# Copies of k's last keys move from ScalarE to GpSimd, with six weight loads behind them in GpSimd's queue

## The chip, the cores and the metric

The kernel runs on one core of a Trainium2 chip. The metric is the device time of one execution in microseconds (us). Engines are named as the profile names them: PE is TensorE's matmul, PEld its weight load, DVE VectorE, ACT ScalarE, POOL GpSimd, SP SyncE. SP, ACT and POOL can issue DMAs; SPq, ACTq and POOLq are their queues. L331 is line 331 of the kernel before.

## What is computed

An attention with a threshold over 8 batches, 8 heads, 576 positions and 64 channels, in float32, and after it a feed-forward over all 4608 rows:

```
scores = q k^T / 8;  thresh = max(scores) - tau      (per row)
scores = where(scores >= thresh, scores, -1e9)
attn = softmax(scores);  a = attn v
x = a with heads side by side: (4608, 512)
h = x w_in;  g = h * sigmoid(1.702 h);  out = g w_out   (w_in 512 x 2048, w_out 2048 x 512)
```

The weights arrive in float64. The core has to make float32 of them itself.

## The kernel before, in words

**Pairs.** Two heads of a batch are worked together, so there are 32 pairs, counted from 0. A pair's 576 keys are four tiles of 128 and a tail of 64. For the four tiles the scores of each head are products of its own (`scores`, L350). For the tail both heads share one product: `prep_kd` (L331) copies the last 64 keys of each head's transposed k into the two diagonal 64x64 blocks of `kd`, a 128x128 tile whose other blocks were zeroed once at the start (L597), and the product with `kd` (L343) gives the tail scores of both heads. There is a single `kd`, so the copies of a pair wait until the tail product of the pair before has read it.

**A pair's way.** SP issues 4 DMAs for q and 4 for k of 72 KB each (`load_qk`, L220; for pair 0 ACT issues k's) and 4 for v (`load_v`, L230 and L234). q and k are read in rows of 32 floats, and their buffers are single; pairs 1 and 3 have buffers of their own inside `gT`, so names like gT<-in_q_dram or gT<-ps are theirs. DVE transposes q and k (`prep`, L326). PE makes the scores, ACT copies them out of PSUM (`keep`, L369), DVE takes the maxima in groups (`in_groups`, L383), folds them (L389 to L423) into one row. For the first eight pairs SP writes that row to DRAM (`row_out`, L435) and reads it back into all partitions as `mb` and `mbt` (`row_in`, L444 and L446). DVE subtracts it (`sub`, L453, L455), ACT masks and takes the exponential (L464, L468), PE multiplies by v (`values`) and, for the first five pairs, by ones for the sums (`sums_by_pe`, both L482), DVE divides (L511 to L532) and places the result in `xT` (L549).

**Weights.** There are 32 pieces of 128x512, 16 of w_in and 16 of w_out. POOL issues two DMAs of 512 KB for each (`load_w`, L278 and L279; the second is shifted by three bytes), and DVE and ACT make float32 of a piece in four steps: the exponent on DVE (`cv_ex`, L289), a power of two on ACT (`cv_power`, L297), the fraction on DVE (`cv_frac`, L303, L307), the product on DVE (`cv_end`, L315). Pieces are staged in parts of `w_out` that are free until later, or in two pairs of buffers w64; each load waits for its place to be given back by a `cv_end`, once the six places have been used.

**Feed-forward.** For blocks of 512 rows PE makes 16 tiles of h (`mm1`, L561), ACT a tanh (L569), DVE the gate (L572), then PE the second product (`mm2`, L580), ACT halves it (L587) and SP stores it. Its matmuls fill PE between the pairs' work, and the last blocks follow after the last pair.

**The order.** The order on each engine is fixed when the program is built. Each step is a `task` with an engine, a supposed cost, a rank, the tasks it comes `after`, and the pools it takes and gives. `run_in_order` plays these with supposed times and writes each engine's instructions in the order in which they would start. What an engine waits for on the chip is another thing: an instruction waits there only for data that it reads or overwrites, and for the instructions ahead of it on its engine. So the loads of pieces 0 to 5, which overwrite nothing that anyone still reads, are placed after a transpose in the plan (the lines with `w_loads` below), and on the chip have only the order of POOL before them. A planned wait holds the chip only where something ahead on the same engine really waits.

On POOL that order is, before: memsets, the load of tau, then the 32 weight loads. On ACT each pair's two copies stand ahead of its score copies or among them.

```
        if n in (2, 3):

            for a in w_loads[3 * (n - 2) : 3 * (n - 1)]:
                tasks[a][5].append(pk)
        pd = task("ACT", 0.5, r, prep_kd, n, after=[pk], take=("kd",))
```

`pk` is the transpose of k, `pd` the copies into `kd`; `tasks[a][5]` is the list of what load `a` comes after.

Of the kernel before, what the change touches and what calls it, by code (L numbers as in the profile page):

```python
# [30 lines left out]
def kernel(  # L31
# [29 lines left out]
    nc = tc.nc  # L61
# [29 lines left out]
    kd = const.tile([P, P], FP32, name="kd")  # L91
# [15 lines left out]
    tasks = []  # L107
# [26 lines left out]
    def task(engine, cost, rank, f, *a, after=(), take=(), give=(), lag=0.06):  # L134
        if 0 <= rank < LAST:
            rank += CV.get(f.__name__, 0.0) + (EARLY if a[0] < 2 * NPAIR else LATER).get(f.__name__, 0.0)
        tasks.append((engine, cost, rank, f, a, [x for x in after if x is not None],
                      take, give, lag))
        return len(tasks) - 1
# [67 lines left out]
    def own(n, *pools):  # L207
        return tuple(x + "_apart" for x in pools) if n in APART else pools
# [119 lines left out]

    def prep_kd(n):
        for h in range(2):  # L330
            nc.scalar.copy(  # L331
                out=kd[ts(h, D), ts(h, D)], in_=mats[n, 1][ts(h, D), MAIN:S]
            )

# [298 lines left out]
    for i in range(len(pieces)):  # L633
# [6 lines left out]
        a = task("POOL", 2.4, rank, load_w, i, after=w_loads[-1:], take=place, lag=5.0)  # L640
# [3 lines left out]
        a = task("DVE", 1.14, rank, cv_frac, i, after=[e])  # L644
# [47 lines left out]
    for n in range(NP):  # L692
        gate = per_pair * (n - LEAD)
        after = ffn[gate : gate + 1] if gate >= 0 else []
        r = float(n)
# [6 lines left out]
        lv = task("SP", 2.1, r - 1.2, load_v, n, take=("v_m", v_tail), lag=2.0)  # L702
        pq = task("DVE", 0.77, r, prep, n, 0, after=[lq], take=own(n, "qkT0"), give=own(n, "raw0"))
        pk = task("DVE", 0.77, r, prep, n, 1, after=[lk], take=own(n, "qkT1"), give=own(n, "raw1"))
        if n in (2, 3):

            for a in w_loads[3 * (n - 2) : 3 * (n - 1)]:
                tasks[a][5].append(pk)
        pd = task("ACT", 0.5, r, prep_kd, n, after=[pk], take=("kd",))
        mx = []  # L710
        for t in range(NKT + 1):
            tail = t == NKT
            copies = []
            for c in range(1 if tail else 2):

                a = task(
                    "PE", (0.97 if tail else 0.53) * slow, r, scores, n, t, c,
                    after=[pq, pk] + ([pd] if tail else []) + after,
                    take=("psA", "s_t") if tail else ("psA",) + (own(n, "s_m") if c == 0 else ()),
                    give=own(n, "qkT0", "qkT1") + ("kd",) if tail else (),  # L720
                )
                after = [a]
                copies.append(task("ACT", 0.65, r, keep, n, t, c, after=[a], give=("psA",)))
            mx.append(task("DVE", 0.76 if tail else 1.37, r, in_groups, n, t, ALU.max, after=copies))
        a = task("DVE", 0.78, r, over_tiles, n, ALU.max, after=mx)
        a = task("DVE", 0.78, r, over_groups, n, ALU.max, after=[a])
        if n < BY_DMA:
            a = task("DVE", 0.5, r, lower_rows, n, after=[a, tau_done], take=("row",))
            a = task("SP", 0.35, r, row_out, n, after=[a], lag=2.8)
# [4 lines left out]
        else:  # L734
            a = task("DVE", 0.7, r, lower, n, after=[a, tau_done])
            m = task("DVE", 1.38, r, spread_max, n, after=[a], take=own(n, "mb"))
        ws, subs = [], [m]
        for t in range(NKT + 1):
            tail = t == NKT
            a = task(  # L740
                "DVE", (0.76 if n < BY_DMA else 1.5) if tail else 1.36, r, sub, n, t, after=subs[-1:],
                give=own(n, "mb") + (("mbt",) if n < BY_DMA else ()) if tail else (),
            )
            subs.append(a)
            a = task("ACT", 0.68 if tail else 1.16, r, mask, n, t, after=[a])
# [3 lines left out]
        if n < NPAIR:  # L749

            pv = den = None
            for t in every:
# [3 lines left out]
                    take=("psM", "psM") if first else (),  # L756
# [3 lines left out]
                    take=("psA",) if first else (), give=(back[t],) if t < NKT else ("s_t", "v_m", v_tail),  # L760
                )
            a = task("DVE", 1.22, r, one_row, n, after=[den], give=("psM", "psM"))
        else:
            pv = task("PE", 4.85, r, values, n, every, after=ws + [lv], take=("psA",), give=("v_m", v_tail))
        if NPAIR <= n < BY_PE:
            a = task("PE", 5.2, r, sums_by_pe, n, every, False, after=ws + [pv], take=("psA",), give=back)
            a = task("DVE", 1.22, r, one_row, n, after=[a], give=("psA",))
        elif n >= BY_PE:
# [4 lines left out]
            a = task("DVE", 0.78, r, over_tiles, n, ALU.add, after=su + [pv], give=back)  # L773
            a = task("DVE", 0.78, r, over_groups, n, ALU.add, after=[a])
            a = task("DVE", 0.7, r, one_group, n, after=[a])
        a = task("DVE", 1.07, r, spread_sums, n, after=[a], take=("rc",))
# [41 lines left out]
```

## Time and profile before

| what | value |
|---|---|
| runs shown | 1429.61, 1431.24, 1432.67 us (median 1431.24) |
| the profiled execution | 1432.38 us; its span from the first to the last instruction 1430.5 us |
| mean granted clock of TensorE | 0.989 |
| PE busy | 1383.7 us (97%) |
| DVE busy | 970.2 us (68%) |
| ACT busy | 662.9 us (46%) |
| POOL busy | 36.8 us (3%) |
| copies into kd on ACT | 128, median 0.243 us |
| weight loads, issue on POOL | 64 DMAs, about 0.54 us each |
| weight loads, issue to landing | 8.4 us (median of w_in's first parts) |
| q and k loads of SP, issue to landing | 2.2 and 2.3 us (medians) |

The profile is of one execution. Busy time is the time in which an engine carried out instructions; an idle engine that is not on the path to the end costs nothing. A line of the timeline or of the chain of waits gives the start and the length in us; where several instructions stand in one line, the length reaches over all. "SPq L220" in the chain means that the path went through SP's issuing of that DMA. In the rows of the DMA queues a share is the time that packets took, of the time of all 16 DMA engines.

### The profile page before, as it was taken

The numbers are of one execution on the slowest core, as the hardware profiler recorded it, in microseconds if no ns is written. First come the engines' busy times: TensorE is split into PE (matmuls) and PEld (weight loads), VectorE is DVE, ScalarE is ACT, GpSimd is POOL, SyncE is SP. The second block draws the span as 40 slices with busy tenths as digits, with TensorE's granted clock in tenths as the row PEclk, the third lists the DMA queues.
The fourth block names the chain that finished last, engine by engine and source line by source line (L and its number), as shares of the span: only waits on it lengthen the run. The fifth ranks groups of instructions, "written<-read, shape, count | busy, mean of one in ns | idle before, by whom it ended". The sixth has DMA issues, their size and how long they took to land.

```text
span 1430.5 us, 13702 instructions
## 1 busy us (share of the span) xinstructions
PE 1383.7 (97%) x4936; PEld 652.2 (46%) x4936; DVE 970.2 (68%) x1629; ACT 662.9 (46%) x886; POOL 36.8 (3%) x78
## 2 busy tenths in 40 slices
PE   4779999999999999999999999999999999999998
PEld 2434444444444444444444444444444444444443
DVE  3999899988878887788788887888778710100200
ACT  3786555755555555555555555555445500100100
POOL 2012210000000000000000000000000000000000
PEclk8899999999999999999999999999999999999999
DMA  9476962211111111111111111111110000000000
GB/s 246 92 216 219 308 199 65 74 26 25 33 40 33 26 25 40 40 25 25 33 40 33 26 25 40 41 25 25 33 40 8 1 7 22 0 7 22 0 7 22
DMA packets 205707, 79.31 MB, mean 55 GB/s; under 512 B 192840, under 2 KB 192840, under 8 KB 205640
## 3 DMA queue, kind: packets, MB, share of 16 engines
q1 hardware_dynamic: 196072, 44.60, 14.5%
q0 software_dynamic: 7200, 33.55, 6.5%
q8 instruction: 39, 0.64, 0.2%
q10 hardware_dynamic: 2368, 0.30, 0.2%
q14 instruction: 28, 0.23, 0.1%
HBM read 68.93 MB, written 9.47 MB: 55 GB/s over the span
## 4 chain that ended last, share of the span: by engine, by line
PE 88%; DVE 6%; SPq 2%; DMA 2%; ACT 2%; issue 1%; DVEq 0%; ACTq 0%
PE ops L580 34%; PE hps L561 34%; PE pv L482 9%; PE ps L350 8%; PE ps L343 2%; SPq L220 2%; DVE part L383 1%; DVE s_m L453 1%; DMA mb<-row 1%; ACT gT L468 0%; DVE gT L453 0%; PE den L482 0%; DMA row<-flat 0%; ACT gT L464 0%; DVE part_t L383 0%
## 5 line engine op out<-in xcount | busy, mean ns | idle before, releaser
L561 PE MATMUL hps<-xT,w_in 128*128 128x512 f32 x1152 | 505.7, 595 | 1.9 <-DVE gT L572 1.9
L580 PE MATMUL ops<-w_out,gT 128*128 128x512 f32 x1152 | 506.6, 595 | 0.0
L383 DVE TRANSPOSE_TENSOR_REDUCE part<-s_m 128x36 f32<-128x1152 f32 x228 | 303.9, 1360 | 98.9 <-ACT s_m L369 92.2
L561 PEld LDWEIGHTS hps<-xT,w_in 128*128 128x128 f32 x1152 | 216.3, 190 | 269.4 <-issue 254.3
L580 PEld LDWEIGHTS ops<-w_out,gT 128*128 128x128 f32 x1152 | 216.1, 190 | 268.3 <-issue 265.9
L572 DVE SCALAR_TENSOR_TENSOR gT<-th,hps 128x512 f32<-128x512 f32 x144 | 97.7, 678 | 234.7 <-ACT th L569 233.9
L369 ACT COPY s_m<-ps 128x576 f32<-128x576 f32 x240 | 139.2, 651 | 173.0 <-PE ps L350 171.7
L569 ACT ACTIVATE th<-hps 128x512 f32<-128x512 f32 x144 | 85.3, 592 | 205.7 <-PE hps L561 194.0
L464 ACT ACTIVATE s_m<-s_m 128x1152 f32<-128x1152 f32 x120 | 138.6, 1155 | 72.5 <-DVE s_m L453 72.3
L468 ACT ACTIVATE s_m<-s_m,shift,scl 128x1152 f32<-128x1152 f32 x120 | 161.8, 1348 | 2.9
L453 DVE TENSOR_TENSOR s_m<-s_m,mb 128x1152 f32<-128x1152 f32 x120 | 156.4, 1351 | 7.1 <-DMA mb<-row 6.5
L350 PE MATMUL ps<-qkT 64*128 64x288 f32 x960 | 144.8, 433 | 13.7 <-DVE qkT L326 12.2
L350 PEld LDWEIGHTS ps<-qkT 64*128 64x128 f32 x960 | 84.0, 190 | 91.6 <-issue 51.5
L482 PE MATMUL pv<-s_m,v_m 128*64 128x288 f32 x960 | 124.2, 411 | 0.0
L587 ACT ACTIVATE osb<-ops 128x512 f32<-128x512 f32 x36 | 21.4, 593 | 220.8 <-PE ops L580 220.8
L482 PEld LDWEIGHTS pv<-s_m,v_m 128*64 128x64 f32 x960 | 67.1, 137 | 63.4 <-issue 10.7
L383 DVE TRANSPOSE_TENSOR_REDUCE part_t<-s_t 128x18 f32<-128x576 f32 x59 | 44.1, 747 | 1.6 <-ACT s_t L369 0.8
L549 DVE TENSOR_TENSOR xT<-pv,rc 128x288 f32<-128x288 f32 (+8 forms) x96 | 28.4, 352 | 17.3 <-PE pv L482 16.6
L343 PE MATMUL ps<-qkT,kd 128*128 128x288 f32 x120 | 36.9, 430 | 0.0
L482 PE MATMUL pv<-s_t,v_t 128*64 128x288 f32 x256 | 36.5, 406 | 0.0
L458 DVE TENSOR_TENSOR s_t<-s_t,mb 64x576 f32<-64x576 f32 x48 | 36.0, 750 | 0.3
L427 DVE STREAM_TRANSPOSE mb<-thr 128x1152 f32<-128x1152 f32 x24 | 33.1, 1378 | 0.8
(81 smaller groups left out, 611.8 us busy)
## 6 DMA issues: line engine op xcount, KB each, us to landing
out_dram<-osb SPq DMA_DIRECT2D x36, 256.0 KB, 2.0
q_raw<-in_q_dram SPq DMA_DIRECT2D x120, 72.0 KB, 2.2
k_raw<-in_k_dram SPq DMA_DIRECT2D x116, 72.0 KB, 2.3
v_m<-in_v_dram SPq DMA_DIRECT2D x64, 128.0 KB, 2.3
w_out<-in_moe_w_in_dram POOLq DMA_DIRECT2D x12, 512.0 KB, 8.4
w<-in_moe_w_out_dram POOLq DMA_DIRECT2D x12, 512.0 KB, 5.7
w_out<-in_moe_w_in_dram POOLq DMA_DIRECT2D x12, 511.6 KB, 9.2
w64s<-in_moe_w_out_dram POOLq DMA_DIRECT2D x12, 511.6 KB, 6.8
```

Of the source, the lines that this page charges most:

```text
L343: nc.tensor.matmul(ps[:, i, 0:SH], lhsT=kd, rhs=qT[:, ts(i, SH)], start=True, stop=True,)
L350: nc.tensor.matmul(ps[:, h, 0:SH], lhsT=kT[ts(h, D), ts(t, P)], rhs=qT[ts(h, D), ts(c, SH)], start=True, stop=True,)
L369: nc.scalar.copy(out=o, in_=pss.pop((n, t, c))[:, :, 0:SH])
L383: nc.vector.tensor_reduce(out=o, in_=i, axis=AXL.X, op=op, apply_transpose=True)
L453: nc.vector.tensor_tensor(out=s, in0=s, in1=mb, op=ALU.subtract)
L464: nc.scalar.activation(out=s, in_=s, func=AF.Prelu, alpha=STEEP)
L468: nc.scalar.activation(out=s, in_=s, func=AF.Exp, scale=scl, bias=shift)
L482: nc.tensor.matmul(o[c][ts(h, D), 0:SH], lhsT=lhsT, rhs=rhs, start=(t == 0), stop=(t == NKT),)
L561: nc.tensor.matmul(hidden[j], lhsT=w_in[:, c, ts(j, P)], rhs=xTs[blk][:, c, :], start=(c == 0), stop=(c == NDC - 1),)
L569: nc.scalar.activation(out=ths[j], in_=hidden[j], func=AF.Tanh, scale=GELU_SCALE / 2)
L572: nc.vector.scalar_tensor_tensor(out=gT[j], in0=ths.pop(j), scalar=1.0, in1=hidden.pop(j), op0=ALU.add, op1=ALU.mult)
L580: nc.tensor.matmul(acc[i], lhsT=gT[j][:, ts(i, P)], rhs=w_out[:, j, :], start=(j == 0), stop=(j == NFC - 1),)
```

## The change

`prep_kd` is carried out by POOL, as a tensor copy, in place of ACT. In the plan its task is one of POOL's, with the same supposed cost, and it is made ahead of the lines with `w_loads`; the loads of pieces 0 to 2 now come after the copies of pair 2, those of pieces 3 to 5 after the copies of pair 3, where they came after the transposes of k of these pairs.

```diff
     def prep_kd(n):
         for h in range(2):
-            nc.scalar.copy(
+            nc.gpsimd.tensor_copy(
                 out=kd[ts(h, D), ts(h, D)], in_=mats[n, 1][ts(h, D), MAIN:S]
             )
...
         pk = task("DVE", 0.77, r, prep, n, 1, after=[lk], take=own(n, "qkT1"), give=own(n, "raw1"))
+        pd = task("POOL", 0.5, r, prep_kd, n, after=[pk], take=("kd",))
         if n in (2, 3):
 
+
             for a in w_loads[3 * (n - 2) : 3 * (n - 1)]:
-                tasks[a][5].append(pk)
-        pd = task("ACT", 0.5, r, prep_kd, n, after=[pk], take=("kd",))
+                tasks[a][5].append(pd)
```

In the built program POOL's order becomes: memsets, tau, the copies of pairs 0, 1 and 2, the loads of pieces 0 to 2, the copies of pair 3, the loads of pieces 3 to 8, the copies of pair 4, pieces 9 to 18, pair 5, pieces 19 to 29, pair 6, pieces 30 and 31, and then the copies of pairs 7 to 31. The second copy of a pair waits for the first. PE's and SP's orders are the same as before. On DVE one reduction (L383) of pair 5 stands behind five instructions of weight conversion that it stood ahead of; on ACT one score copy changes places with one step of conversion; else only the copies are gone there.

## Prediction

> **What bounds the kernel now.** I read the busy time by stage first, because the shares of the whole span (PE 97%) hide where the 3% lies. The columns are the stretch, its length, busy time with instructions of PE, PEld, DVE, ACT and POOL, granted clock, DMA share, GB/s.
>
> ```profile
> 0.00:45.00 45.00, 21.12 (x104) 14.03 (x104) 18.82 (x32) 18.55 (x34) 8.26 (x26) 0.89 0.88 231
> 45.00:122.00 77.00, 60.81 (x390) 31.99 (x392) 73.83 (x133) 62.37 (x72) 10.61 (x20) 0.87 0.58 172
> 122.00:200.00 78.00, 76.15 (x232) 34.90 (x234) 70.81 (x124) 41.55 (x61) 17.89 (x32) 1.00 0.79 251
> 200.00:1150.00 950.00, 949.00 (x3562) 449.04 (x3560) 782.47 (x1304) 514.08 (x676) 0.00 (x0) 1.00 0.16 35
> ```
>
> From 122 us on PE is busy 1025 of 1028 us: nothing is to be had there. From 45 to 122 VectorE is full (73.8 of 77). In the first 45 us no engine is (PE 21, DVE 19, ACT 19), and the DMA share is 0.88. PE's idle time before 122 us is 23.9 + 16.2 = 40.1 us, the cap of any gain. What holds the head stands in the chain of waits up to 46 us (start, length, what):
>
> ```profile
> 6.62 0.70 SPq L220
> 7.32 0.04 issue
> 7.36 7.56 SPq L220
> 14.93 0.04 issue
> 14.97 6.59 SPq L220
> ...
> 26.11 2.38 DMA gT<-in_k_dram
> ...
> 37.75 1.67 DMA row<-flat
> 39.42 0.02 issue
> 39.44 5.32 DMA mb<-row
> ```
>
> SP needs 15.5 us, from 6.62 to 22.15, to issue the four q loads of pair 1 (pairs are counted from 0), where four loads of the next pair take 2.06. Everything on the head's path is behind SP's queue: pair 1's k, the row of pair 0's maxima, and its broadcast mb, on which DVE starts its first subtract at 44.78. The DMA queues say why. Two windows (queue, packets, MB, share of 16 engines), first 6 to 22 us, then 24 to 38:
>
> ```profile
> q0 software_dynamic: 1234, 5.75, 93.8%
> q1 hardware_dynamic: 1139, 0.28, 8.3%
> ```
>
> ```profile
> q1 hardware_dynamic: 13165, 1.78, 75.6%
> ```
>
> q0 holds POOL's weight loads, q1 SP's loads. Beside the weights q1 moves 1139 packets in 16 us, 71 a us; alone 13165 in 14 us, 940 a us. A 72 KB load of q or k is cut into 128 byte pieces, 576 of them: 0.6 us alone, 8 us beside the weights. The weights come that early because the first six loads wait for nothing but their queue (POOL's timeline: start, length, operation):
>
> ```profile
> 2.46 0.53 POOL L278 DMA_DIRECT2D w_out<-in_moe_w_in_dram  x1
> ```
>
> while DVE first touches them at 69 us (DVE's timeline, the first conversion):
>
> ```profile
> 69.05 0.39 DVE L289 TENSOR_SCALAR w_out<-w_out 128x512 uint32<-128x512 uint32 x1
> ```
>
> **The change part by part.** *The order.* Before, "after pk" tied the first loads to a DVE transpose in the planner alone: the order on POOL had nothing ahead of them, so they ran at 2.46. Now POOL's order is copies of pairs 0, 1, 2, loads 0 to 2, copies of pair 3, loads 3 to 5. Those copies wait for DVE's transpose of k and for the tail scores of the pair before (PE), and POOL works in order: the loads are now held on the chip.
>
> *Head without weights.* SP starts the q loads of pair 1 at 6.62 as before. From there to the row are 28 issues (q, k of pairs 1, 2, 3 and v of pair 1). From 26.71 to 37.75, without weights, 20 issues took 11.04, 0.552 each: 28 x 0.552 = 15.5, so SP is ready for the row at 22.1, not 37.75. Is the row's data there? The loads of pair 0 (4608 packets, two queues) at 940 a us from about 2 us are in by about 7; k was transposed at 11.35 before. PE then starts at about 7.5 (12.19 before), ACT's last score copy ends 9.0 later (12.19 to 21.20), 16.5; the last large reduction (1.34) and the fold from 31.84 to 34.70 (2.9) give 20.7. SP at 22.1 is last: **-15.6** for the row.
>
> *First burst.* Pair 2's transposes follow the fold in DVE's order (1.44), so its copies on POOL start at 22.2, also behind the tail scores of pair 1 (PE, about 7.5 + 2 x 8.3 = 24 at the pace of pairs 0 and 1, a score copy every 0.96 us; 21 if pair 2's pace, eight in 4.45, comes sooner). So loads 0 to 2 issue from 22.7 to 24.7 on; an issue at 2.46 became heavy traffic some 2.2 later (156 GB/s from 2.5 to 5 us, 253 and 335 in the next two stretches of 2.5), so at 25 to 27. They are 3.1 MB, at the 379 GB/s of the window from 6 to 22 us about 8.2 us. The row goes out at 22.1 and mb is issued at 23.8: the row escapes, mb does not. Prices from rows: row 1.67 alone and 4.28 beside weights (at 155.53), mb 5.32 alone and 7.33 beside weights (at 159.83). I take 1.7 + 7.3: mb at 31.1, not 44.75, **-13.7**. The ends are -15.6 (neither is hit) and -11.0 (both are).
>
> *Second burst.* Loads 3 to 5 come after the tail scores of pair 2, which end at 62.93 now: at 49.2, plus copies, 50 to 53, on the wires from 52 to 60.5. Beside them stand pair 5's loads, issued at 68.50 to 73.73 before, 55 to 60 now: mostly starved until 60.5, then 4.9 us for 4608 packets, to 65.4. The row of pair 2 (77.34, so 63.6) queues behind them on SP's queue, up to 1.8 late. Its cover: mb was issued at 78.57, took 3.7 (median of that window), and DVE came to it at 84.41, 2.1 later. So it may cost nothing; up to 5 if the cover is gone. I take **+0.7**.
>
> *Are the weights late?* Load 0 is due at 69.05, so 55.4, and lands by 36. Load 3 is due at 73.25, so 59.6; issued at 50, with 8.4 us to landing (median of these loads) at 58.4. It is covered by 1 us at worst; loads 4 and 5 are due at 97. What is late next there is load 3, at its lateness, on DVE.
>
> *The copies themselves.* 128 copies of 64x64 leave ACT: 128 x 0.243 = 31 us of 663. ACT is busy 514 of 950 us in the long stage and PE 949, so this is worth 0; the copies' own waiters lost 3.0 us in four places of PE's weight loads, with 1.0 us of PE idle in that stage: at most 1. The trace has no POOL copy: a POOL memset of 64x64 is 0.144, POOL's longest row 0.76. A pair costs 0.3 to 1.5; I take 0.5, as on ACT (the same shape). It is hidden wherever eight score products stand between the transpose and the tail (137.76 to 145.51 for pair 5). On POOL the copies stand behind loads: those of pair 5 behind load 18 (139.28, 6 us before PE wants them), of pair 6 behind load 29 (189.3, wanted at 215.3), of pair 7 behind load 31 (199.9, wanted at 242.4). In the other direction load 9 waits behind pair 4's copies, which wait for PE at 84.8; it went out at 97.80. All 0 now; without that cover each us is one of PE's.
>
> The Trainium skill speaks against this place: SBUF — State Buffer, section "Who interferes with whom", says that a DVE instruction with two SBUF inputs contends with a GpSimd instruction that reads SBUF, and that whoever comes second is fully blocked. No row here shows it. By the rule a copy could wait out one subtract (1.35 us, row of L453), or hold DVE for its own length: under 1 us in the head, and in the long stage against 6 us of cover; the sum would be -12, not -13.
>
> *DVE's order.* One reduction of pair 5 slides behind five instructions of weight conversion near 197 us, 2.9 us by their rows, with PE full: 0, at most 3.
>
> *Does the shift last?* DVE does the same work from the first subtract on and is full until 122 us; PE after that. Weight loads from the seventh on wait for DVE's conversions (65.8 us of POOL's waiting) and move with them. So the whole rest is moved forward.
>
> **Sum.** -13.7 + 0.7 = -13.0. The profiled execution took 1432.38 (span 1430.5): 1419.4. The median of the runs, 1431.24, lies 1.14 lower: **1418.2**.
>
> **Rivals.** (1) *The bursts cost more than I price.* For: 71 against 940 packets a us, and only 1 to 2 us of room on either side. If row and mb are both hit (-11.0) and the second burst costs its 5: -6 , 1425. Against: the weights need over 2 us from issue to traffic. (2) *The head's gain is covered up.* DVE could be stopped after 45 us by something that doesn't move: the conversions, fed by loads that now queue behind PE and DVE. For: POOL waits for both now. Against: only loads 0 to 5 changed, and they are due late. Time 1431. That the order doesn't hold the loads would also end here, but POOL has one queue. (3) *Slower: the starved queue.* If pair 3's last k load still has its 576 packets to move when the weights arrive, they need 8.1 us at 71 a us, ahead of row and mb; with both hit (+4.6) and pair 5's loads starved on the path for the whole second burst (+8.2) that is 20.9 against 15.6: +5.3, 1436.5. It decides at about 1.5 us: SP issues that load by 22, its packets go within 2, the weights come at 25 to 27. (4) *Better.* POOL's copies come late enough (27) to spare mb altogether, and cold products of pair 1 run at pair 2's pace: -17, 1414.
>
> **Chances.** Forecast (1415.5 to 1420.5) 0.66; rival (1), 1420.5 to 1426, 0.19; (4) 0.06; (2) 0.05; (3) 0.04. A measurement of this kernel tells 0.2% (2.9 us) from no change. Faster by more than that 0.91, within 0.05, slower 0.04. The range goes from 1414, the end without contention (-15.6) and the 1.6 by which the lowest run lies under the median, to 1425, the end of (1).
>
> **What would show it.** Right: in the changed profile the q loads of pair 1 take about 2 us on SP, first row at about 22, first subtract at 30 to 32, POOL's first weight load at 22 to 26, mb at 7 rather than 5 us, PE's idle before its first hps some 13 lower, the long stage unchanged. Wrong: a row or mb above 10 us, DVE idle ahead of a conversion (L289, L303), PE idle ahead of L343 with the copy as releaser, or a first subtract after 36.

## The result and the profile after

The changed kernel took 1425.13 us (median of four runs, 1422.51 to 1427.46) against 1431.36 for the kernel before: a ratio of 0.9957, interval 0.9933 to 0.9981. It is 6.2 us faster, where I forecast 13.0, and its time lies 0.1 above my range. In a later comparison of the same kernel (e8 below) the median was 1420.05 against 1432.57 for the kernel before, 12.5 us faster, and its runs went from 1416.72 to 1426.49. So this kernel's time is spread over 11 us, where those of the kernel before stay within 3 to 5, and the question has two parts: where do up to 12 us go, and why not in every run?

The profiled execution shown here is the slowest of the four, 1427.46 us with a span of 1425.7, against 1432.38 and 1430.5 before. First the busy time by stage, with the columns of the prediction (PE, PEld, DVE, ACT, POOL, granted clock, DMA share, GB/s):

```profile
0.00:45.00 45.00, 28.73 (x174) 16.98 (x176) 33.30 (x54) 27.71 (x38) 6.45 (x26) 0.92 0.84 181
45.00:122.00 77.00, 50.50 (x333) 25.46 (x330) 61.74 (x116) 51.73 (x61) 15.44 (x30) 0.89 0.71 214
122.00:200.00 78.00, 78.00 (x261) 36.33 (x261) 72.61 (x130) 39.25 (x55) 19.21 (x36) 1.00 0.80 261
```

The head did what was forecast: in the first 45 us DVE works 33.3 us instead of 18.8. But in the next stretch, where DVE was full (73.8 of 77), it now works only 61.7. Twelve us that the head won are lost there. The chain of waits says on what (start, length, what):

```profile
21.16 2.17 DMA row<-flat
23.34 6.24 DMA mb<-row
29.60 1.37 DVE s_m L453
...
52.72 0.70 DVE qkT L326
53.44 8.58 DMA q_raw<-in_q_dram
...
66.26 0.51 DVE w_in L315
66.78 11.06 DMA row<-flat
77.85 3.99 DMA mb<-row
81.86 1.50 DVE s_m L453 x2
```

The row of pair 0 leaves SP at 21.16 instead of 37.75, and DVE starts its first subtract at 29.60 instead of 44.78. The new entry is the row of pair 2, 4.5 KB, which needs 11.06 us. DVE's timeline shows its price (start, length, operation; in brackets the idle time before it and what ended it):

```profile
29.60 5.17 DVE L453 TENSOR_TENSOR s_m<-s_m,mb 128x1152 f32<-128x1152 f32 x4 [1.60 <-DMA mb<-row]
...
81.86 5.17 DVE L453 TENSOR_TENSOR s_m<-s_m,mb 128x1152 f32<-128x1152 f32 x4 [12.45 <-DMA mb<-row]
```

Pair 0's subtract is 15.2 us earlier than before, pair 2's only 2.55 (84.41 before, with no wait for mb there). The difference, 12.6, is the wait of 12.45. The same steps in the kernel before, from the timelines of SP, POOL and DVE:

```profile
77.34 0.28 SPq L435 DMA_DIRECT2D row<-flat  x1
78.57 0.36 SPq L444 DMA_DIRECT2D mb<-row  x1
80.24 0.54 POOL L278 DMA_DIRECT2D w_out<-in_moe_w_in_dram  x1 [65.81 <-DVE w_in L315]
84.41 5.13 DVE L453 TENSOR_TENSOR s_m<-s_m,mb 128x1152 f32<-128x1152 f32 x4
```

What stands beside that row in the changed kernel is in POOL's timeline, and in the DMA queues from 66.8 to 77.8 us (queue, packets, MB, share of 16 engines):

```profile
65.16 0.54 POOL L278 DMA_DIRECT2D w_out<-in_moe_w_in_dram  x1 [12.93 <-DVE w_in L315]
```

```profile
q0 software_dynamic: 659, 3.09, 78.0%
q1 hardware_dynamic: 1252, 0.15, 9.3%
```

Piece 6, and 7 and 8 behind it, are issued when DVE's conversions give back their places. That was at 80.24 before, after row and mb of pair 2 (77.34 and 78.57). Now it is at 65.16, before the row. And the 1252 small packets on SP's queue are mostly what was left of pair 5's four k loads, 2304 packets that stand ahead of the row in the same queue; at 114 packets a us beside the weights that rest takes the 11 us.

One more view tells why PE's idle time in total says little here: groups of PE's instructions with mean duration and idle time before them, first of before, then of after.

```profile
L350 PE MATMUL ps<-qkT 64*128 64x288 f32 x960 | 144.8, 433 | 13.7 <-DVE qkT L326 12.2 <-ACT s_m L369 1.0 <-DVE xT L549 0.6
L482 PE MATMUL den<-s_m,ones 128*64 128x288 f32 x96 | 17.0, 496 | 10.3 <-ACT s_m L468 10.3
L350 PE MATMUL ps<-gT 64*128 64x288 f32 x64 | 11.8, 523 | 9.9 <-DVE gT L326 9.0 <-DVE xT L549 0.6 <-ACT gT L369 0.3
```

```profile
L350 PE MATMUL ps<-qkT 64*128 64x288 f32 x960 | 144.0, 431 | 10.3 <-DVE qkT L326 9.0 <-ACT s_m L369 0.7 <-DVE xT L549 0.6
L482 PE MATMUL den<-s_m,ones 128*64 128x288 f32 x96 | 17.4, 506 | 22.3 <-ACT s_m L468 22.3
L350 PE MATMUL ps<-gT 64*128 64x288 f32 x64 | 9.2, 427 | 0.9 <-DVE xT L549 0.6 <-ACT gT L369 0.3
```

PE's waits for the transposes of q and k fall from 21.2 us (12.2 and 9.0) to 9.0: the loads of pair 1 are no longer starved. Its waits for the masked scores of ACT, which follow DVE's subtract, rise from 10.3 to 22.3. The gain was made and given back on the same engine.

### The profile page after: what moved, and what is told of

Read it like the earlier page. It is cut to its first block, busy times and chain, and to the rows that moved or that the text cites. A ratio compares the mean times of both kernels' runs of the same rounds, so it can differ in the third digit from the quotient of the medians.

```text
span 1425.7 us, 13775 instructions
## 1 busy us (share of the span) xinstructions
PE 1378.0 (97%) x4936; PEld 647.3 (45%) x4936; DVE 970.6 (68%) x1629; ACT 646.5 (45%) x822; POOL 52.8 (4%) x142
## 4 chain that ended last, share of the span: by engine, by line
PE 92%; DMA 3%; DVE 2%; ACT 2%; SPq 1%; issue 1%; ACTq 0%; DVEq 0%
PE ops L580 35%; PE hps L561 35%; PE pv L482 10%; PE ps L350 9%; PE ps L343 2%; DMA row<-flat 1%; DMA q_raw<-in_q_dram 1%; DMA mb<-row 1%; SPq L220 1%; PE den L482 1%; DVE s_m L453 0%; ACT s_m L468 0%; DVE part L383 0%; ACT s_m L464 0%; ACT gT L464 0%
## 5 line engine op out<-in xcount | busy, mean ns | idle before, releaser
L383 DVE TRANSPOSE_TENSOR_REDUCE part<-s_m 128x36 f32<-128x1152 f32 x228 | 303.8, 1360 | 97.4 <-ACT s_m L369 91.1
L350 PE MATMUL ps<-qkT 64*128 64x288 f32 x960 | 144.0, 431 | 10.3 <-DVE qkT L326 9.0
L482 PEld LDWEIGHTS pv<-s_m,v_m 128*64 128x64 f32 x960 | 66.8, 137 | 63.8 <-issue 10.1
L331 POOL COPY kd<-qkT 64x64 f32<-64x64 f32 x60 | 14.0, 234 | 913.2 <-DVE qkT L326 909.8
L383 DVE TRANSPOSE_TENSOR_REDUCE part_t<-s_t 128x18 f32<-128x576 f32 x59 | 44.1, 747 | 1.6 <-ACT s_t L369 0.8
L482 PE MATMUL den<-s_m,ones 128*64 128x288 f32 x96 | 17.4, 506 | 22.3 <-ACT s_m L468 22.3
```

The source lines that it names most:

```text
L350: nc.tensor.matmul(ps[:, h, 0:SH], lhsT=kT[ts(h, D), ts(t, P)], rhs=qT[ts(h, D), ts(c, SH)], start=True, stop=True,)
L383: nc.vector.tensor_reduce(out=o, in_=i, axis=AXL.X, op=op, apply_transpose=True)
L482: nc.tensor.matmul(o[c][ts(h, D), 0:SH], lhsT=lhsT, rhs=rhs, start=(t == 0), stop=(t == NKT),)
```

## The experiments

My theory after this profile: two bursts together cost the 12 us. The second (pieces 3 to 5) holds pair 5's loads back, so that pair 2's row leaves late and has unsent packets ahead of it; the third (pieces 6 to 8), which came forward with DVE, then starves the queue in which that row waits. Against it stand: that the copies on POOL cost the time; that the second burst costs it by itself; and that the wait, taken away, only comes back at the next place. (Where an expectation names a rival by a letter, what follows it says in words which of these fell.)

**e1: the copies on POOL, the loads where they were.**

```diff
     def load_w(i):
+        if i in early:
+            return
...
+    for i in range(6):
+        load_w(i)
+        early.add(i)
     run_in_order()
```

> Copies on POOL, but the first six loads stand ahead of them in POOL's queue, as before; the orders of the other engines are those of the changed kernel. Theory (bursts: the hold of the loads makes the whole difference, in the head for the better, between 53 and 82 us for the worse): the time of before, 1431 within 2, first subtract near 44. Rival A (the copies on POOL cost time that the hold's gain pays for): slower than before, by about the 7 us that the forecast lacks, 1437 to 1439.

Measured: 1430.14 (11 runs, 1428.86 to 1433.52), ratio 0.9992, interval 0.9984 to 1.0001. Row of pair 0 at 38.11, as before. 31 us of work that leave ACT for POOL change nothing that can be measured: the gain is all in the place of the weight loads, and neither gain nor loss is in the copies.

**e2: the loads held, the copies on ACT.** Two memsets of a block of zeros of `kd` stand in POOL's queue ahead of the loads instead of the copies.

```diff
+    def hold(n):
+        nc.gpsimd.memset(kd[ts(0, D), ts(1, D)], 0.0)
...
+        pd = task("ACT", 0.5, r, prep_kd, n, after=[pk], take=("kd",))
+        held = []
+        if n in (2, 3):
+            held = [task("POOL", 0.5, r, hold, n, after=[pk] + after[:1])]
```

> Copies stay on ACT; the loads of pieces 0 to 2 and 3 to 5 are held on POOL by two memsets of a zero block of kd that wait for the tail scores of pair 1 and of pair 2. Theory: as the changed kernel, 1422 to 1427, first subtract near 30, row of pair 2 taking about 10 us. Rival A: the gain without the copies' cost, 1416 to 1419. Rival B (it was leaving ACT that shortened the head): no gain, 1431.

Measured: 1424.31 (1423.52 to 1425.2), ratio 0.9949, interval 0.9937 to 0.9961. The second memset did not wait for the tail product of pair 2, as my expectation has it (it stands ahead of that product in the program), so the six loads left one after another from 22.55 us on, with DVE waiting 8.64 us for pair 1's row: the shape of e4 and not that of the changed kernel. It shows that loads held without any copy on POOL gain as much; for the changed kernel's own shape e5 had to be built.

**e4: all six loads behind the copies of pair 2** (no second burst).

```diff
-        if n in (2, 3):
-            for a in w_loads[3 * (n - 2) : 3 * (n - 1)]:
+        if n == 2:
+            for a in w_loads[:6]:
                 tasks[a][5].append(pd)
```

> The changed kernel with all six loads behind the copies of pair 2, so that the second burst joins the first. Theory: the same loss at another place: pair 4's loads starve until about 42 and pair 1's row stands behind them, leaving near 47 in place of 40.7; the first subtract of pair 1 at 52 to 54 in place of 46.1; then pair 5's loads are free of weights, pair 2's row leaves within 1 us of its fold and takes about 2, mb meets pieces 6 to 8 in part. In all 1421 to 1426. Rival C: pieces 3 to 5 come earlier, so faster than the changed kernel by what DVE waited for them: under 1 us by its profile, 1424.

Measured: 1423.9 (1423.12 to 1425.72), ratio 0.9947, interval 0.9935 to 0.996. SP's timeline (start, length, operation):

```profile
24.64 14.75 SPq L220 DMA_DIRECT2D q_raw<-in_q_dram  x4
39.43 9.99 SPq L220 DMA_DIRECT2D k_raw<-in_k_dram  x4
49.52 0.36 SPq L435 DMA_DIRECT2D row<-flat  x1
...
71.51 0.28 SPq L435 DMA_DIRECT2D row<-flat  x1
72.73 0.36 SPq L444 DMA_DIRECT2D mb<-row  x1
```

and DVE's:

```profile
55.34 2.63 DVE L453 TENSOR_TENSOR gT<-gT 128x1152 f32<-128x1152 f32 x2 [9.20 <-DMA gT<-row]
```

Now the double burst starves pair 4's loads (24.7 us of issuing), pair 1's row leaves at 49.52 instead of 40.66, and DVE waits 9.2 us there. The same loss stands one pair earlier. At the other place, pair 2's row takes 1.2 us and DVE doesn't wait for it, though the third burst follows at 74.41: a burst alone, behind row and mb, costs nothing.

**e3: the third burst held.** A POOL copy of one column of pair 2's mb stands ahead of piece 6, so pieces 6 to 8 leave when mb has landed.

```diff
+    def behind_mb(n):
+        nc.gpsimd.tensor_copy(out=seen, in_=mbs[n][:, 0, 0:1])
...
+        if n in {2: 6}:
+            g = task("POOL", 0.3, r, behind_mb, n, after=[m])
+            tasks[w_loads[{2: 6}[n]]][5].append(g)
```

> The changed kernel with one more copy on POOL ahead of the load of piece 6, which reads one column of pair 2's mb, so pieces 6 to 8 go out only when that mb has landed. Theory: pair 2's row still leaves at about 66.8 (held up behind pair 5's loads), but takes 2 us in place of 11 and its mb 4 to 5; first subtract of pair 2 at 73 to 74 in place of 81.9, and the end 6 to 9 earlier, 1416 to 1419. Rival C (the loss is DVE waiting for weights that come late): pieces 6 to 8 come later still, so 1425 or more.

Measured: 1419.57 (1416.47 to 1419.98), ratio 0.9913, interval 0.9899 to 0.9926; the profiled execution is the fastest, 1416.47. SP's timeline, then DVE's:

```profile
58.30 5.76 SPq L221 DMA_DIRECT2D k_raw<-in_k_dram  x4
64.17 0.58 SPq L439 DMA_DIRECT2D row<-flat  x1
66.05 0.36 SPq L448 DMA_DIRECT2D mb<-row  x1
```

```profile
70.25 5.16 DVE L457 TENSOR_TENSOR s_m<-s_m,mb 128x1152 f32<-128x1152 f32 x4
```

The second burst is still there, and the row still leaves 1.0 us after DVE has folded it (63.15); but the row takes 1.9 us, mb 3.9, and pair 2's subtract starts at 70.25 with no wait, 14.2 earlier than before. DVE is busy 72.2 of 77 us from 45 on. 12.1 of the forecast 13.0 are there. So the second burst by itself isn't the cost, and the wait doesn't come back elsewhere.

**e5 and e6: is POOL needed for the copies at all?** e5 is the changed kernel's order with copies on ACT; two memsets on POOL hold the loads, each waiting for the tail product of the pair before. e6 adds e3's gate, the POOL copy that holds piece 6 until mb has landed.

```diff
+            held = [task("POOL", 0.5, r, hold, n, after=[pk, tail_scores])]
...
+                tail_scores = a
```

> Copies back on ScalarE; in their place on POOL two memsets of the zeros beside pair 2's and pair 3's copies, each waiting for the tail product of the pair before, so that POOL's order is hold, loads 0 to 2, hold, loads 3 to 5, as in the changed kernel. Theory (the weight loads' new place makes the whole difference, the engine of the copies nothing): pair 2's row is again caught between loads 3 to 5 and 6 to 8, takes about 11 us, and DVE waits about 12 for mb; 1422 to 1428, as the changed kernel (1425.1). Rival (the copies on POOL, 1.2 us beside DVE's subtracts, cost some of the gain): 1418 to 1421.

> The kernel of e5 with load 6 held, by a POOL copy of one column of pair 2's mb, until that mb has landed. Theory: row of pair 2 takes 1.5 to 2 us, no wait of DVE for it above 2, time as that of e3 (1416 to 1420), so the move of the copies to POOL isn't needed for any of the gain. Rival (the copies off ScalarE are worth something once DVE's wait is gone): 1421 to 1424.

Measured: e5 1422.7 (1417.34 to 1427.31), ratio 0.993, interval 0.9909 to 0.9951; e6 1418.5 (1417.1 to 1422.56), ratio 0.9912, interval 0.9896 to 0.9928. Both medians are where the theory had them; e6 is e3 with the copies on ACT. But e5's profiled execution, 1418.41, doesn't show the 11 us that I expected of it. From its chain of waits:

```profile
64.01 1.86 DMA row<-flat
65.88 5.79 DMA mb<-row
```

The row left at 64.01, 1.7 us ahead of piece 6 (65.71), and escaped. So the theory needed an addition: in this shape row and third burst leave within 2 us of each other, and small delays from run to run decide which is first. That predicts the same spread for the changed kernel, and a time that follows the row.

**e8, e9, e10: does the time follow the row from run to run?** The changed kernel twice more, and e5's once more, unedited.

> The changed kernel once more. The runs of e5 spread from 1417 to 1427, and the profiled one, 1418.4, has a row of pair 2 of 1.9 us, while the changed kernel's profiled run, 1427.5, has one of 11. Theory: it is decided from run to run whether the row gets out ahead of loads 6 to 8, since row and loads leave within 2 us of each other. So its runs should spread over some 1418 to 1428, and the profiled one should follow its row: about 1427 with a row near 11 us, 1417 to 1421 with one below 3. Rival (a lasting difference between copies on POOL and holds on POOL): all runs above 1422, the row near 11 us.

> The changed kernel, one more profile. Theory and rival as for e8: the time follows the row of pair 2, about 1427 with a row near 11 us, 1417 to 1421 with one below 3; in between in proportion.

> The kernel of e5 once more, one more profile. Theory: time follows the row of pair 2, about 1426 with a row near 11 us, 1417 to 1420 with one below 3. Rival (this kernel's spread has another cause): a time above 1422 with a short row, or below 1420 with a long one.

Measured: e8 1420.05 (six runs, 1416.72 to 1426.49), ratio 0.9913, interval 0.9895 to 0.9931, its profiled execution 1424.7; e9 1419.8; e10 1424.21. From the chains of waits of e8, then of e10:

```profile
65.43 3.24 DMA row<-flat
...
68.69 9.03 DMA mb<-row
```

```profile
64.73 1.95 DMA row<-flat
66.69 9.71 DMA mb<-row
```

All profiled executions of this shape and the two with the gate, in order of time; the columns are where the row left, how long it took, where mb left, when piece 6 was issued, DVE's wait for that mb, and the time without that wait:

| execution | time | row | took | mb | took | piece 6 | DVE's wait | without |
|---|---|---|---|---|---|---|---|---|
| changed | 1427.46 | 66.78 | 11.06 | 77.85 | 3.99 | 65.16 | 12.45 | 1415.0 |
| e8 (changed) | 1424.70 | 65.43 | 3.24 | 68.69 | 9.03 | 65.46 | 8.03 | 1416.7 |
| e10 (holds) | 1424.21 | 64.73 | 1.95 | 66.69 | 9.71 | 65.30 | 6.88 | 1417.3 |
| e9 (changed) | 1419.80 | 64.48 | 1.92 | 66.41 | 6.05 | 65.87 | 2.37 | 1417.4 |
| e5 (holds) | 1418.41 | 64.01 | 1.86 | 65.88 | 5.79 | 65.71 | 1.74 | 1416.7 |
| e6 (holds, gate) | 1417.10 | 64.45 | 1.88 | 66.34 | 3.80 | 71.51 | 0 | 1417.1 |
| e3 (changed, gate) | 1416.47 | 64.17 | 1.9 | 66.05 | 3.9 | 70.58 | 0 | 1416.5 |

The last column spans 2.4 us where the first spans 11: one wait carries the spread of the profiled executions. The wait follows the margin, from when the row leaves to when piece 6 is issued: -1.62, 0.03, 0.57, 1.39 and 1.70 us in the five without the gate, with waits of 12.45, 8.03, 6.88, 2.37 and 1.74; the kernel before has 2.90 and no wait. That the runs without a trace follow it too is taken from there, not shown. The rival's sign for e10, a time above 1422 with a short row, did come true; but there it was mb, not the row, that met the weights, 9.71 us instead of 3.8, and DVE's wait tells it. e8, 1424.70 with a row of 3.24 us and an mb of 9.03, is the same case. My theory had named only the row. The rival of a lasting difference between copies and holds on POOL is out: four of e8's six runs lie under 1422. In e3 and e6 the rows left as early as in e5 and e9, which lost 1.7 and 2.4 us without the gate; so these two executions show no more than that as the gate's own doing, and the rest of their lead over 1427.46 is an earlier row.

**e7: the gate one place earlier,** ahead of piece 4: only piece 3 is left in the second burst. The edit is that of e3 with `{2: 4}`.

> The changed kernel with the gate one place earlier: load 4 (and so 5 to 8 behind it in POOL's order) waits for pair 2's mb, and only load 3 is left in the second burst. Theory (the second burst only delays pair 2's row by some 2 us, which the work queued on DVE covers; the third burst is what costs): row of pair 2 leaves about 62.5 instead of 64 to 67, and the time is that of e3, 1416 to 1420, within 1 us of it in the same call's terms. Rival (the second burst costs 2 us or more by itself): 1413 to 1416. Second rival (loads 4 to 8 now come too late for DVE's conversions, or all five fall on the rows of pair 3): 1421 or more.

Measured: 1419.92 (1418.47 to 1420.5), ratio 0.9913, interval 0.9901 to 0.9925, the same as e3. Row of pair 2 at 63.21, mb at 64.43, and pair 2's subtract at 70.28, where it was in e3: until then DVE has other work. What is left of the second burst in e3 costs nothing. The five loads behind mb are felt a pair later, where DVE waits 2.9 us for pair 3's mb (a small form of the second rival; in DVE's timeline):

```profile
91.61 3.90 DVE L457 TENSOR_TENSOR gT<-gT 128x1152 f32<-128x1152 f32 x3 [2.92 <-DMA gT<-row]
```

e3 and e6 beat the kernel before. Against the changed kernel their eleven runs together have a median of 1419.57 where its own eleven have 1422.51, but these come from different comparisons, and e8's ratio is that of e3, 0.9913: a gain in the median isn't shown. What the gate takes away is the slow end: one of its eleven runs is above 1422.5 (1422.56), and six of the changed kernel's, up to 1427.46.

## Why the prediction was wrong, point by point

- **Head without weights: right.** SP's row at 21.16 (forecast 22.1), q loads of pair 1 in 2.06 us on SP.
- **First burst: right.** Pieces 0 to 2 issue from 22.98 (22.7 to 24.7); the row escapes; mb takes 6.24 (7.3). First subtract at 29.60 (31.1): -15.2 where I took -13.7 (-16.8 in e8, -16.6 in e9), and up to -16.9 in e3 (27.85).
- **Second burst, +0.7: its lateness was more than I said, its price less.** The row of pair 2 leaves 1.0 (e3) to 4.5 us (changed kernel, 62.23 to 66.78) after its fold, where I said up to 1.8; the price by itself is 0 (e3, e6, e7). My "up to 5 if the cover is gone" is no bound on what followed.
- **The step that failed** is in the paragraph on whether the shift lasts: "Weight loads from the seventh on wait for DVE's conversions and move with them. So the whole rest is moved forward." They do move with DVE, by 15.1 us (80.24 to 65.16). But pair 2's row hangs on SP's queue behind pair 5's loads, which the second burst holds, and moved by only 10.6 (77.34 to 66.78). In the kernel before, row and mb left 2.9 and 1.7 us ahead of piece 6; that order was a margin and I never wrote it down as one. The missing term is 1.7 to 12.5 us of DVE's waiting in the five profiled executions of this shape. I had priced two bursts and not looked for a third. The prediction's own numbers held the meeting: moved by 13.7, piece 6 stands at 66.5 and the row at 63.6 to 65.4, so that mb, 1.7 later, is issued between 1.2 us ahead of piece 6 and 0.6 behind it. One of its signs of being wrong came true, a row above 10 us.
- **The chance.** Rival (1), 1425 at 0.19, had the right direction but the wrong place: it added the row of pair 0 and the second burst's own 5. Neither happened, so that its 1425 lies next to the first median, 1425.13, is luck. So is in part the 12.5 us of e8's comparison, near my 13.0: by the executions with a trace, 15.2 to 16.8 us were won at the first subtract, and a wait that I had put at nothing, 2.4 to 12.5 us, was paid out of them.
- **The copies: right.** 0 for ACT's 31 us (e1: -1.1 us by its ratio, interval -2.3 to +0.1; e6 against e3: ratios of 0.9912 and 0.9913).
- **The contention that I weighed from the Trainium skill** (SBUF — State Buffer, "Who interferes with whom"): the traces now agree. A pair's two copies take 0.53 us alone, and 1.28 in the changed kernel's profile for pair 3, 1.64 in e8, beside subtracts with two SBUF inputs (46.09 to 48.64, and from 46.40); in e9, where the copies started at 46.38 and the subtract at 46.80, 0.53. The subtracts are hardly longer (2.63 and 2.67 us for two, 2.63 in e9). On the path this is at most 1.1 us of later second burst: e8's pieces 3 to 5 left at 47.80 and its row at 65.43, e9's at 46.88 and 64.48. That it pushed e8 to the wrong side is only argued; e10 was pushed there with no copy on POOL at all.
- **Weights late: right,** none. DVE's waits for a conversion are 0.5 us, as before.

What decides from run to run where between 64.0 and 66.8 the row leaves is open in part. In the seven executions of the table it leaves 16.8 to 17.7 us after the second burst starts with piece 3: at 49.05 in the slowest, 47.80 in e8, and 46.54 to 47.24 in the others. So a second burst that comes 2 us later, behind a later tail product or slower copies, passes this on to the row; that is read from these executions, and no run moved that issue alone. Also open are two of e6's six runs, 1421.35 and 1422.56, with the gate in place: neither has a trace. A kernel in which the row goes out ahead of pair 5's loads on SP's queue was not tried.

## What to carry to other kernels

When a change moves one chain forward, list every transfer that leaves near it, and move each by its own releaser: two that were 2 us apart on different engines can change places. Write the margin between them down as a term with a price, as one does with a wait. Price a small transfer beside a burst by what stands ahead of it in its queue and not by its own size (here 4.5 KB took 1.2 to 11.06 us), or hold the burst until the small transfer has landed (e3 and e6: one POOL copy, 0.18 us in e3 and 1.37 beside a subtract in e6, and the slowest run is 1422.56 instead of 1427.46).

## What the hardware showed that I had not expected

- A row of 4.5 KB takes 1.2 us alone (e4), 1.9 with some of pair 5's loads ahead of it, and 11.06 with over a thousand of their packets ahead and weights beside; mb, 576 KB, takes 3.8 to 4.0 alone and 9.0 to 9.7 beside a whole burst.
- From 6 to 22 us in the kernel before, q1 moved 1139 packets beside 1234 of q0; in the changed one from 66.8 to 77.8 us 1252 beside 659. The Trainium skill (DMA: Bandwidth & Descriptors, "Queues, rings and completion order") says that each DMA engine goes round the queues that have work, a packet at a time. If the profile's packets are the page's, 0.9 small packets to a large one agrees with that, and so does the changed kernel where the weights fill the engines: from 71.8 to 75.8 us, with q0 at 98.3%, 350 packets beside 328. The 1.9 comes from stretches with less of the weights: from 68.8 to 71.8 us, with q0 at 75.1%, 641 beside 155.
- PE's busy time fell with the head: 1383.7 to 1378.0 us for the same 4936 matmuls. The scores from `gT` take 427 ns each instead of 523, 2.6 us of busy time in that group alone. Those of pair 1 started from 29.5 to 36.2 us before, where the granted clock was 0.61 (29.5 to 37 us); now they start from 16.5 to 20.5 us, with 1.00 (16.5 to 22.5 us).
- A copy of 64x64 float32 on POOL is 0.234 us (median of 60), on ACT 0.243.
